# A quarter of wq's odd rows loaded behind wq's main part, by transfers of 95 and 33 partitions

## The chip, the cores and the metric

The kernel runs on one core of a Trainium2 chip. The metric is the device time of one execution in microseconds; the figure for a kernel is the median over several rounds. Profiled executions are single executions with the hardware profiler on.

## The reference

One decode step of a transformer block: layer norm, attention of one query token over a window of a cache, projection and residual, then layer norm, a gated feed-forward part with a relu gate, and residual. Four sequences, D = 576, 32 query heads on 16 key/value heads, head size 128, a window of 4096 positions, F = 4608, all in bf16.

```python
def _A_ref(x, k_cache, v_cache, wq, wo):
    W = min(4096, max(256, Sk // 4))                       # 4096
    q = (x @ wq).reshape(B, 1, 32, 128).transpose(0, 2, 1, 3)
    k = jnp.repeat(k_cache[:, :, Sk - W:, :], 2, axis=1)
    v = jnp.repeat(v_cache[:, :, Sk - W:, :], 2, axis=1)
    p = _softmax(jnp.einsum("bhqd,bhkd->bhqk", q, k) * (128 ** -0.5))
    o = jnp.einsum("bhqk,bhkd->bhqd", p, v)
    return o.transpose(0, 2, 1, 3).reshape(B, 1, 32 * 128) @ wo

def _B_ref(x, W_gate, W_up, W_down):
    gate = x @ W_gate
    return ((gate * (gate > 0)) * (x @ W_up)) @ W_down

h = A_x + _A_ref(_layernorm(A_x), A_k_cache, A_v_cache, A_wq, A_wo)
out = h + _B_ref(_layernorm(h), B_W_gate, B_W_up, B_W_down)
```

## The kernel before

Every input is read once: about 160 MB, of which 134 MB are K and V. The work on K and V is cut into 16 quads, each of one sequence and four key/value heads. A quad of K or of V is one transfer of 128 partitions with 32 KB each.

**Buffers.** All big inputs go through one SBUF tensor, `pool`, with four slots of 32 KB a partition. The helper `add` (from line 204) appends a transfer to the list `transfers` and notes who used the same bytes before it; the transfer waits for those users. Slots are handed out in turn to K0, K1, V0, K2, V1, K3 and so on.

**wq.** `wq` has 576 rows of 4096 columns. Rows 0 to 511, the main part, go as one transfer of 128 partitions with 32 KB each into slot 2 (`("wq", 0)`, line 237). Rows 512 to 575, called the odd rows here, are cut in halves of 2048 columns, so that they fill 128 partitions with 4 KB each: row r, half u stands in partition 2r + u. They go at the beginning of slot 3 (`("wq", 4)`, line 235) and are the first transfer in the list. V0 takes slot 2 and K2 slot 3 afterwards, and so both wait for the query projection (`QMM`).

**SP issues the list in order** (`prog_sync`): odd rows, main part, K0, K1, V0, K2 and so on, then `wo`, the gate and up weights, and six transfers of W_down. An issue whose buffer isn't free holds up all issues behind it. The sixteen DMA engines of the core work off what SP has issued, one row after the other; each transfer has a semaphore, which its engines raise as their shares land. x alone is issued by ACT.

**PE** (`prog_pe`, loop at line 483) computes the query projection in five blocks of contraction, the odd rows first (`c == 4`), then the four blocks of the main part. Each block is eight matmuls of 512 columns, and the accumulation over the five blocks ends with `QMM`. The first matmul of block 4 waits for the landing of the odd rows and for `XN41`, the normalized x that goes with them; the first of block 0 waits for the main part. ACT then copies the result into `q_bf` (line 311), and DVE transposes that (line 427, behind the first K transpose on line 403), from which the queries of the quads are made.

**The quads.** DVE transposes K in four parts (line 403), PE multiplies it with the queries, DVE and ACT make the softmax, PE multiplies with V, DVE collects. K2's and later loads wait for the transposes of the K that stood there, V's slots for the matmuls with V.

Line 466 is the helper for a matmul that loads its weights, line 468 the one for a matmul that keeps them.

Of the kernel before, what the change touches and what calls it, by code (L numbers as in the profile page):

```python
# [30 lines left out]
QUAD = NS * WIN * DH // 128  # L31
# [70 lines left out]
def bass_sequential_preLN__sliding_block_cached__glu_gated_reglu__decode_kernel(  # L102
# [12 lines left out]
    with ExitStack() as es:  # L115
        cnt = [0]

        def sb(name, shape, dt):
            return es.enter_context(nc.sbuf_tensor(name, shape, dt))

        pool = sb("pool", [128, NSLOT * QUAD], BF16)
# [79 lines left out]
        transfers = []  # L201
        at = {}

        def add(name, key, off, n, consumer, make):

            free = []
            for u in list(users):
                if u[0] < off + n and off < u[1]:
                    if u[2] not in free:
                        free.append(u[2])  # L210
                    if off <= u[0] and u[1] <= off + n:
                        users.remove(u)
            users.append((off, off + n, consumer))
            at[name] = off
            transfers.append((name, key, free, lambda e: make(e, pool[:, off:off + n])))
# [7 lines left out]
        def add_K(i):  # L223
            x = next(slots) % NSLOT
            add(("K", i), f"slot{x}", x * QUAD, QUAD, ("TR", 4 * i + 3),
                lambda e, o: e.dma_start(out=o, in_=quad(A_k_cache, i)))

        def add_V(i):
            x = next(slots) % NSLOT
            add(("V", i), f"slot{x}", x * QUAD, QUAD, ("PV", i),  # L230
                lambda e, o: e.dma_start(out=o, in_=quad(A_v_cache, i)))

        HQ = H * DH

        add(("wq", 4), "wq4", 2 * QUAD + 4 * HQ, HQ // 2, "QMM",
            lambda e, o: e.dma_start(out=o, in_=A_wq[512:576, :].rearrange("r (u n) -> (r u) n", u=2)))
        add(("wq", 0), "wq0", 2 * QUAD, 4 * HQ, "QMM",
            lambda e, o: e.dma_start(out=o, in_=A_wq[0:512, :].rearrange("(p u) n -> p (u n)", u=4)))
        for m in range(NQUAD + VLEAD):
            if m < NQUAD:  # L240
                add_K(m)
            if m >= VLEAD:
                add_V(m - VLEAD)
        add(("wo",), "wo", 0, EO * D, "ATTN",
            lambda e, o: e.dma_start(out=o, in_=A_wo.rearrange("(p e) n -> p (e n)", e=EO)))
        for k, (kind, W) in enumerate((("wg", B_W_gate), ("wu", B_W_up))):
            add((kind, 0), f"{kind}0", GU0 + 4 * k * ROW, 4 * F, None,
                lambda e, o, W=W: e.dma_start(out=o, in_=W[0:512, :].rearrange("(p u) n -> p (u n)", u=4)))
            add((kind, 4), f"{kind}4", GU0 + 8 * ROW + k * HALF, HALF, None,
                lambda e, o, W=W: e.dma_start(out=o, in_=W[512:576, :].rearrange("r (u n) -> (r u) n", u=2)))  # L250
# [3 lines left out]
        for k, (f0, f1) in enumerate(WD):  # L254
            transfers.append((("wd", k), f"wd{k}", ["ATTN"],
                              lambda e, f0=f0, f1=f1: e.dma_start(
                                  out=pool[:, f0 * D:f1 * D], in_=B_W_down.rearrange("(p j) n -> p (j n)", j=JJ)[:, f0 * D:f1 * D])))
# [4 lines left out]
        def land(name):  # L262
            return ("L",) + (name if isinstance(name, tuple) else (name,))
# [195 lines left out]
        def prog_pe(S):  # L459
            t = "tensor"  # L460

            def mm(o, l, r, start, stop, deps=(), name=None, skip=False, held=False):

                def make(e):
                    if not held:
                        return e.matmul(o, lhsT=l, rhs=r, start=start, stop=stop, skip_group_check=skip)  # L466
                    tile = tuple(next(x for x in (32, 64, 128) if x >= n) for n in (l.shape[0], l.shape[-1]))
                    return e.add_instruction(mybir.InstMatmult(  # L468
                        name=nc.get_next_instruction_name(), start_tensor_calc=start, stop_tensor_calc=stop, bass_skip_group_check=skip,
                        tile_size=tile, tile_position=(0, o.offset // o.ap[0][0] % 128), ldweights=False,  # L470
                        ins=[e.lower_ap(r), e.lower_ap(l)], outs=[e.lower_ap(o)]))

                S.op(t, make, deps=deps, name=name, signal=name is not None)
# [8 lines left out]
            mm(pb[STB][:, 0:B], dup[:, :], x4[:, :], True, True, deps=["D_X4", "DUP"], name="XDUP")  # L482
            for c in (4, 0, 1, 2, 3):
                s = at[("wq", 0)] + c * HQ if c < 4 else at[("wq", 4)]
                deps = [land(("wq", 0)), "D_XNT"] if c == 0 else [land(("wq", 4)), "XN41"] if c == 4 else []
                for g in range(4):
                    x0 = s + (g if c < 4 else g % 2) * 1024
                    for k in range(2):
                        mm(pb[QB[k]][32 * g:32 * g + 32, :], xnT[:, c, :] if c < 4 else xn4[:, g // 2, :], pool[:, x0 + 512 * k:x0 + 512 * k + 512], c == 4, c == 3,
                           deps=deps, name="QMM" if c == 3 and g == 3 and k == 1 else None, skip=True, held=k == 1)  # L490
                        deps = []
            for g in range(4):
                mm(pb[g][:, 0:128].rearrange("p (x h b) -> p x h b", x=4, b=B), sel[32 * g:32 * g + 32, :, :].rearrange("p g k -> p (g k)"),
                   qT[32 * g:32 * g + 32, :].rearrange("p (h x b) -> p x h b", x=4, b=32)[:, :, :, 0:B], True, True,
                   deps=["D_QT", "SEL"] if g == 0 else [], name="QREP" if g == 3 else None)
# [57 lines left out]
            for q in range(4):  # L553
                mm(pb[0][:, 0:EO * B], spread[:, q, :, :].rearrange("p h k -> p (h k)"), o_bf[:, q * EO:(q + 1) * EO, :].rearrange("p e b -> p (e b)"), q == 0, q == 3,
                   deps=["NORM", "SPREAD"] if q == 0 else [], name="OSEL" if q == 3 else None)
            for e_ in range(EO):
                deps = [land(("wo",)), "OX"] if e_ == 0 else []
                for u in range(2):
                    c0 = at[("wo",)] + e_ * D + u * HD
                    mm(attn[:, u * HD:(u + 1) * HD], oX[:, e_, :], pool[:, c0:c0 + HD], e_ == 0, e_ == EO - 1,  # L560
                       deps=deps, name="ATTN" if e_ == EO - 1 and u == 1 else None, held=u == 1)
                    deps = []
# [10 lines left out]
            for u, kind in ((0, "wg"), (1, "wu")):  # L573
                if u == 1:
                    residual()
                for c in range(4):
                    s = at[(kind, 0)] + c * F
                    deps = [land((kind, 0))] + (["N2"] if c == 0 and u == 0 else [])
                    for k, (f0, f1) in enumerate(CUTS):
                        for q in range(4):  # L580
# [3 lines left out]
                            deps = []  # L584
                s = at[(kind, 4)]
                deps = [land((kind, 4)), "HN41"]
                for k, (f0, f1) in enumerate(CUTS):
                    for q in range(4):
                        x0 = s + (q % 2) * FQ
                        mm(pb[GUB[u][k]][32 * q:32 * q + 32, 0:(f1 - f0) * JJ], hn4[:, q // 2, :], pool[:, x0 + f0 * JJ:x0 + f1 * JJ],  # L590
                           False, True, deps=deps, name=(("GATE", "GU")[u], k) if q == 3 else None, skip=True, held=k > 0)
                        deps = []

            for k, (f0, f1) in enumerate(WD):
                deps = [land(("wd", k))]
                for f in range(f0, f1):
                    if f % (JJ // 2) == 0:
                        deps = deps + [("HHT", f // (JJ // 2))]
                    for u in range(2):
                        last = f == FC - 1  # L600
                        mm(down(u), hhT[:, f, 0:B], wd_sb[:, f, OUTS[u][0]:OUTS[u][1]], False, last,
                           deps=deps, name="DOWN1" if last and u == 1 else None, skip=True)
                        deps = []

        progs = [("gpsimd", prog_pool), ("sync", prog_sync), ("scalar", prog_act), ("vector", prog_dve), ("tensor", prog_pe)]
        S.begin(False)
        for _, p in progs:
# [32 lines left out]
```

## Time and profile before

| | |
|---|---|
| median of 3 runs | 377.71 us (377.62 to 377.88) |
| profiled execution | 378.56 us |
| its span, first to last instruction | 377.2 us |
| PE matmul busy | 302.2 us, 80% of the span |
| DVE busy | 225.8 us, 60% |
| ACT busy | 53.4 us, 14% |
| read from HBM | 159.58 MB, 423 GB/s over the span |
| q1 (the queue of SP's transfers) | 98.8% of 16 engines' span |
| TensorE clock granted, mean | 0.923 |

The profiled execution's own time is 1.36 us above its span. A share of the DMA queue is the time that its packets took, over sixteen engines times the span. A DMA row of the issue list gives the median time from the issue by SP to the landing; most of it is time in which the transfer stands behind others. The packet records of the trace have the start, length and size of each packet of the DMA engines, but not the engine's number.

### The profile page before, as it was taken

Reading aid. Unit: us, or ns where it says so; the run is one execution under the profiler, and the core shown is the slowest. Engines: PE = TensorE matmul, PEld = TensorE weight load, DVE = VectorE, ACT = ScalarE, POOL = GpSimd, SP = SyncE. Lnnn points to the kernel's source line nnn. Section 1 sums busy time; section 2 is a strip of 40 time slices with the busy share of each in tenths; the row PEclk is TensorE's granted clock in tenths of the full one; section 3 lists DMA queues with packets and bytes.
Section 4 is the critical chain, followed back from the end, with each engine's and each line's share of the span. In section 5 each row is a group of like instructions: output and inputs, shape, how many; then the busy total and the mean of one; then the engine's idle time right before and its main releaser. Section 6 shows DMA issues by size and latency. Waiting matters only on the chain.

```text
span 377.2 us, 2603 instructions
## 1 busy us (share of the span) xinstructions
PE 302.2 (80%) x1432; PEld 73.0 (19%) x772; DVE 225.8 (60%) x165; ACT 53.4 (14%) x140; POOL 5.2 (1%) x15
## 2 busy tenths in 40 slices
PE   0509299969996999499969996899879996968667
PEld 0101022212221222022212221122112121212214
DVE  8046677595849493858476846666675768231230
ACT  2202402110220112002200220020202010101020
POOL 5000000000000000000000000000000000000000
PEclk9999789998999899989989997799959998996988
DMA  8999999999999999999999999999999999999996
GB/s 334 445 445 389 445 440 393 445 440 438 422 424 441 438 434 408 441 441 427 413 440 441 431 427 427 440 434 427 420 441 440 417 424 441 422 432 429 443 404 255
DMA packets 6506, 159.74 MB, mean 423 GB/s; under 512 B 728, under 2 KB 864, under 8 KB 1632
## 3 DMA queue, kind: packets, MB, share of 16 engines
q1 hardware_dynamic: 6488, 159.59, 98.8%
q8 instruction: 8, 0.13, 0.1%
q10 hardware_dynamic: 8, 0.00, 0.0%
q14 instruction: 2, 0.02, 0.0%
HBM read 159.58 MB, written 0.00 MB: 423 GB/s over the span
## 4 chain that ended last, share of the span: by engine, by line
DMA 47%; DVE 29%; PE 20%; ACT 3%; SPq 1%; issue 1%; DVEq 0%
DMA pool<-in_A_k_cache_dram 41%; DVE kT L403 20%; PE sc L466 7%; PE sc L468 6%; DMA pool<-in_B_W_down_dram 5%; DVE acc L420 4%; PE val L466 3%; PE val L468 3%; DVE own_sb L417 2%; DVE probT L414 2%; ACT P L338 2%; PE pb L466 1%; DVE o_bf L442 0%; ACT L338 0%; DVE rmx L406 0%
## 5 line engine op out<-in xcount | busy, mean ns | idle before, releaser
L403 DVE STREAM_TRANSPOSE kT<-pool 128x2048 f32<-128x2048 f32 x64 | 142.8, 2278 | 25.3 <-DMA pool<-in_A_k_cache_dram 24.3
L466 PE MATMUL sc<-kT,qz 128*128 128x512 bf16 x256 | 110.5, 432 | 36.6 <-DVE kT L403 36.3
L468 PE MATMUL sc<-kT,qz 128*128 128x512 bf16 x256 | 109.6, 428 | 0.0
L466 PE MATMUL val<-pool,probT 128*64 128x512 bf16 (+2 forms) x328 | 104.2, 374 | 4.4 <-DMA pool<-in_B_W_down_dram 4.4
L468 PE MATMUL val<-pool,probT 128*64 128x512 bf16 x256 | 96.2, 379 | 0.0
L466 PEld LDWEIGHTS sc<-kT,qz 128*128 128x128 bf16 x256 | 26.7, 104 | 146.5 <-issue 71.1
L466 PEld LDWEIGHTS val<-pool,probT 128*64 128x64 bf16 (+1 forms) x328 | 32.1, 107 | 81.3 <-issue 68.5
L406 DVE TENSOR_REDUCE rmx<-sc 128x1 f32<-128x1024 f32 x16 | 19.6, 1225 | 41.0 <-PE sc L468 41.0
L333 ACT ACTIVATE diag<-spot,rmx 128x16 f32<-128x16 f32 x16 | 4.9, 307 | 234.0 <-DVE rmx L406 234.0
L414 DVE STREAM_TRANSPOSE probT<-P 128x1024 bf16<-128x1024 bf16 x16 | 19.9, 1246 | 21.0 <-ACT P L338 21.0
L338 ACT ACTIVATE P<-sc,bias 128x1024 bf16<-128x1024 f32 x16 | 17.8, 1114 | 21.0 <-DVE bias L409 21.0
L327 ACT COPY qz<-qrep 32x128 bf16<-32x128 bf16 x64 | 18.8, 294 | 0.6
L409 DVE TENSOR_REDUCE bias<-pb 128x1 f32<-128x16 f32 x16 | 2.8, 175 | 23.8 <-PE pb L466 23.8
L420 DVE TENSOR_REDUCE acc<-own_sb 128x128 f32<-128x1024 f32 x8 | 15.2, 1897 | 0.3
L417 DVE TENSOR_TENSOR own_sb<-val,mask 128x1024 f32<-128x1024 f32 x8 | 9.6, 1200 | 7.9 <-PE val L468 7.9
L466 PE MATMUL sc<-pool,oX 128*4 128x288 bf16 x32 | 10.0, 338 | 0.4 <-ACT oX L347 0.4
L468 PE MATMUL sc<-pool,oX 128*4 128x288 bf16 x32 | 9.9, 336 | 0.0
L478 PE MATMUL pb<-ident_b,xn_bf 4*128 4x4 bf16 (+1 forms) x5 | 0.4, 180 | 10.0 <-DVE xn_bf L371 10.0
L466 PE MATMUL sc<-qT,sel 32*128 32x128 bf16 x4 | 0.3, 284 | 9.6 <-DVE qT L427 9.6
L445 DVE TENSOR_TENSOR h_row<-sc,x_bf 4x576 f32<-4x576 f32 x1 | 0.7, 745 | 11.6 <-PE sc L468 11.6
L466 PE MATMUL pb<-diag,same 128*128 128x16 f32 x32 | 6.3, 273 | 1.7 <-ACT diag L333 1.7
L466 PEld LDWEIGHTS pb<-diag,same 128*128 128x128 f32 x32 | 4.8, 188 | 11.8 <-ACT diag L333 7.4
(102 smaller groups left out, 85.7 us busy)
## 6 DMA issues: line engine op xcount, KB each, us to landing
pool<-in_A_k_cache_dram SPq DMA_DIRECT2D x16, 4096.0 KB, 26.8
pool<-in_A_v_cache_dram SPq DMA_DIRECT2D x16, 4096.0 KB, 26.4
pool<-in_A_wo_dram SPq DMA_DIRECT2D x1, 4608.0 KB, 18.3
pool<-in_B_W_gate_dram SPq DMA_DIRECT2D x1, 4608.0 KB, 18.6
pool<-in_B_W_up_dram SPq DMA_DIRECT2D x1, 4608.0 KB, 24.7
pool<-in_A_wq_dram SPq DMA_DIRECT2D x1, 4096.0 KB, 12.7
pool<-in_B_W_down_dram SPq DMA_DIRECT2D x1, 2016.0 KB, 15.0
pool<-in_B_W_down_dram SPq DMA_DIRECT2D x1, 1296.0 KB, 17.7
```

The source lines that it names most:

```text
L327: S.op(a, lambda e, src=src, dst=dst: e.copy(out=dst, in_=src), deps=deps, name=("QZ", i) if g == 3 else None, signal=g == 3)
L333: S.op(a, lambda e, i=i: e.activation(out=diag[:, i % 2, :], in_=spot[:, :], func=ACT.Copy, scale=rmx[:, i % 2:i % 2 + 1]), deps=[("RMAX", ...
L338: S.op(a, lambda e, i=i: e.activation(out=Pb[:, (i % 2) * 1024:(i % 2 + 1) * 1024], in_=sc[:, (i % 2) * 1024:(i % 2 + 1) * 1024], func=ACT ...
L403: S.op(v, lambda e: e.transpose(out=dst, in_=src), deps=deps, name=("TR", f))
L406: S.op(v, lambda e: e.tensor_reduce(out=rmx[:, i % 2:i % 2 + 1], in_=sc[:, (i % 2) * 1024:(i % 2 + 1) * 1024], axis=AX.X, op=ALU.max), dep ...
L409: S.op(v, lambda e: e.tensor_reduce(out=bias[:, i % 2:i % 2 + 1], in_=pb[TPB][:, 16 * (i % 2):16 * (i % 2) + 16], axis=AX.X, op=ALU.min), ...
L414: S.op(v, lambda e: e.transpose(out=pT[i % NPT], in_=Pb[:, (i % 2) * 1024:(i % 2 + 1) * 1024]), deps=[("EXP", i)] + ([("PV", i - NPT)] if ...
L417: S.op(v, lambda e: e.tensor_tensor(out=own_sb[:, :].rearrange("p (x d) -> p x d", d=DH), in0=val[:, :].rearrange("p (x d) -> p x d", d=DH ...
L420: S.op(v, lambda e: e.tensor_reduce(out=acc[:, w % 2, :], in_=own_sb[:, :].rearrange("p (x d) -> p d x", d=DH), axis=AX.X, op=ALU.add), de ...
L445: S.op(v, lambda e: e.tensor_tensor(out=h_row[:, :], in0=attn, in1=x_bf[:, :], op=ALU.add), deps=["ATTN", land("x")], name="H")
L466: return e.matmul(o, lhsT=l, rhs=r, start=start, stop=stop, skip_group_check=skip)
L468: return e.add_instruction(mybir.InstMatmult(name=nc.get_next_instruction_name(), start_tensor_calc=start, stop_tensor_calc=stop, bass_ski ...
```

## The change

The odd rows' first transfer is narrowed from 2048 to 1536 columns of each half (4 KB to 3 KB a partition). The remaining 512 columns (1 KB a partition, 128 KB in all) are loaded behind the main part and ahead of K0, by two transfers: partitions 0 to 94, and partitions 95 to 127. They go to the same place in SBUF as before. The two share one semaphore. The first matmul of block 4 waits for both as well as for the narrowed one. No computation is changed; no other transfer changes its place relative to the rest.

```diff
-        add(("wq", 4), "wq4", 2 * QUAD + 4 * HQ, HQ // 2, "QMM",
-            lambda e, o: e.dma_start(out=o, in_=A_wq[512:576, :].rearrange("r (u n) -> (r u) n", u=2)))
+        wq_odd = A_wq[512:576, :].rearrange("r (u n) -> (r u) n", u=2)
+        OW = HQ // 2
+        OA = OW - 512
+        add(("wq", 4), "wq4", 2 * QUAD + 4 * HQ, OA, "QMM",
+            lambda e, o: e.dma_start(out=o, in_=wq_odd[:, 0:OA]))
         add(("wq", 0), "wq0", 2 * QUAD, 4 * HQ, "QMM",
             lambda e, o: e.dma_start(out=o, in_=A_wq[0:512, :].rearrange("(p u) n -> p (u n)", u=4)))
+        o0 = 2 * QUAD + 4 * HQ + OA
+        add(("wq", 5), "wq5", o0, 512, "QMM", lambda e, o: e.dma_start(out=o[0:95, :], in_=wq_odd[0:95, OA:OW]))
+        transfers.append((("wq", 6), "wq5", [], lambda e: e.dma_start(out=pool[95:128, o0:o0 + 512], in_=wq_odd[95:128, OA:OW])))
         for m in range(NQUAD + VLEAD):
...
-                deps = [land(("wq", 0)), "D_XNT"] if c == 0 else [land(("wq", 4)), "XN41"] if c == 4 else []
+                deps = [land(("wq", 0)), "D_XNT"] if c == 0 else [land(("wq", 4)), land(("wq", 6)), "XN41"] if c == 4 else []
```

## The prediction

> **What bounds the kernel now.** I read the page in the order DMA rows, chain, waits, issues, then the trace's DMA packet and landing records for the one thing that the page does not separate: the sixteen DMA engines. First the page's slices and queues, and the table of stretches:
>
> ```profile
> DMA  8999999999999999999999999999999999999996
> DMA packets 6506, 159.74 MB, mean 423 GB/s; under 512 B 728, under 2 KB 864, under 8 KB 1632
> q1 hardware_dynamic: 6488, 159.59, 98.8%
> q8 instruction: 8, 0.13, 0.1%
> q10 hardware_dynamic: 8, 0.00, 0.0%
> q14 instruction: 2, 0.02, 0.0%
> ...
> 22.00:62.00 40.00, 27.23 (x106) 6.09 (x58) 26.07 (x17) 9.41 (x24) 0.00 (x0) 0.91 0.99 420
> 62.00:120.00 58.00, 51.93 (x220) 11.92 (x113) 42.73 (x27) 7.76 (x21) 0.00 (x0) 0.97 1.01 433
> 120.00:325.00 205.00, 179.79 (x728) 41.06 (x381) 136.37 (x84) 25.07 (x67) 0.00 (x0) 0.92 1.00 431
> ```
>
> The engines of queue q1 never stop between the first row (1.75 us) and the last (374.7 us): 98.8% of sixteen engines' span. PE (302 us) and DVE (226 us) are below that. The chain's end and the waits say the same:
>
> ```profile
> DMA 47%; DVE 29%; PE 20%; ACT 3%; SPq 1%; issue 1%; DVEq 0%
> ...
> 353.78 20.18 DMA pool<-in_B_W_down_dram
> 373.95 0.04 issue
> 374.00 0.70 PE val L466 x7
> 374.70 0.02 issue
> 374.72 0.68 PE val L466 x5
> 375.40 0.02 issue
> 375.42 0.42 DVE out_sb L456
> ```
>
> The last 20 us are a wait for W_down's rows. After the last landing (375.03 us) come two matmuls, a copy and the output, 2.2 us in all. So the end is set by the slowest engine's own list of packets. The engines do not finish together. These are the sixteen part-landings (us) of the last W_down transfer, from the trace's semaphore records:
>
> ```
> 373.16 373.17 373.22 373.23 373.25 373.37 373.73 374.04
> 374.65 374.66 374.68 374.73 374.75 374.76 374.78 375.03
> ```
>
> For K0, at the start, the spread was only 23.28 to 23.62. Each of q8's eight 16 KB packets (56.6, 97.7, 145.0, 188.6, 240.9, 284.6, 331.5 and 360.4 us) throws one engine back, about 1.55 us, each time another one: eight late engines. Seven land at 374.65 to 374.78; one, which already lagged 0.41 us, is last.
>
> **The price of a row**, from the packet records: rows of 2304 B follow each other on an engine at 89.5 ns, rows of 1152 B at 47 ns, so 4.5 ns a row and 0.0369 ns a byte. That is 42 ns for the new 1 KB row and 118 ns for a 3 KB row; the old 4 KB row is measured at 155 ns. A landing packet costs 6 ns.
>
> **wq4's columns 1536 to 2047 leave the first transfer.** Every engine carries eight of its rows: 8 x (155.3 - 117.6) = 0.30 us less for each of the sixteen.
>
> **The two new transfers** bring 128 rows of 1 KB. How 95 and 33 rows are dealt to engines no row shows. Bounds: sixteen even shares (8 or 9 rows and two landing packets, 0.35 to 0.39 us) net +0.05 to +0.09 us; all 128 rows on one late engine net 128 x 0.042 - 0.30 = +5.1 us; none on a late engine, -0.30 us. Nearest are the transfers of 128 rows (8 on each of 16) and x's 4 rows: q10's eight packets are one row and one landing packet on each of four engines. All are equal shares. With equal shares 95 goes as 5 x 19 and 33 as 11 x 3, and I take these. An engine with both carries 22 rows and nets 22 x 42.2 + 12 - 301 = +0.64 us; one with 19 rows nets +0.51; one with 3 rows, -0.17; one with none, -0.30. On the path counts only what the last engine gets. If the five loaded engines are early ones, they have 1.4 us or more in hand (373.25 against 374.65) and absorb 0.64. The last engine then gains 0.17 or 0.30, and its followers 0.25 us ahead gain at least 0.17, so they don't take over. I take **-0.25 us**.
>
> [...]
>
> Which five are they? Two of x's engines can be followed from their landing packets (ends 1.944 and 2.013 us) to their first wq row (1.941 and 2.010) and on, and as far as equal times allow it, neither is among those that the first four 16 KB packets hit. [...]
>
> **SP's queue.** Two more issues stand between wq's main part and K0; an issue there took 0.39 to 0.6 us, so K0 and K1 are issued about 1 us later. K0 was issued 11.8 us and K1 21 us before their first row's turn. Cost nothing; even at 3 us each it would be covered. No other queue changes place.
>
> **The new wait on PE.**
>
> ```profile
> 11.82 0.62 PE L466 MATMUL val<-pool,xn 128*32 128x512 bf16 x4 [0.97 <-ACT xn L308]
> 13.89 0.62 PE L466 MATMUL val<-pool,xnT 128*32 128x512 bf16 x4 [1.02 <-DMA pool<-in_A_wq_dram]
> 17.55 0.54 SPq L231 DMA_DIRECT2D pool<-in_A_v_cache_dram  x1
> 23.64 2.31 DVE L403 STREAM_TRANSPOSE kT<-pool 128x2048 f32<-128x2048 f32 x1 [13.70 <-DMA pool<-in_A_k_cache_dram]
> 25.88 1.20 DVE L427 STREAM_TRANSPOSE qT<-q_bf 128x1024 bf16<-128x1024 bf16 x1
> SPq L231 <- PE pb L468: 14.7, 1, 14.7
> ```
>
> The odd rows' matmuls, first in PE's order, now wait for both new transfers. These follow wq0, whose part-landings of 13.46 to 13.85 come 0.30 earlier; then 22 rows, 0.94 us: landed at 14.1 to 14.5 instead of PE starting at 11.82. All 40 matmuls queue behind (1.7 + 3.6 us, from 11.82 to 13.5 and 13.89 to 17.5), so they end near 19.7, 2.2 later. Two parties wait for them. The copies on ACT (17.56 to 18.63) move to about 20.8, but the transpose that reads them stands behind the first K transpose and starts at 25.88: 5 us in hand. SP's issue of V0 and, behind it, K2 moves from 17.55 to about 19.7; the engines reach V0 at 33.15: 13 us in hand. If either cover were gone the price would be 2.2 us.
>
> **K0's landing** moves by up to +0.64 on the loaded engines and -0.3 on others, and the first K transpose with it, by at most about 0.6 us. Buffers then free later by as much; the tightest issue I found, wo at 319.43 us, was 5.7 us ahead of its turn (325.12). Cost nothing.
>
> **Traffic settling.** Between 20 and 62 us the 32 KB rows, 1213 ns undisturbed, took longer by 0.88 us per engine in all; from 62 to 120 us hardly any of that is left, and later rows are 3 to 4 ns longer each. Setting five engines 0.8 to 0.95 us apart from the others may change this. Bounds: all of it saved, -0.9; doubled, +0.9. I take 0, since no row tells the sign.
>
> **Sum:** -0.25 against the profiled execution's 378.56 us (span 377.2 and 1.36 around it): 378.3. The median of the timed runs, 377.71, lies 0.85 below that execution; the forecast for the median is **377.45**. Within 0.2% (0.75 us, about what a measurement of this kernel can tell from no change) this is no change.
>
> **Rivals.**
> - *A loaded engine is a late one* (the other side). If the five include one of the seven at 374.78 or before, it ends at 375.42: +0.39, 378.1. If they include the last, +0.64, 378.35. It decides from the point where an engine's slack is under 0.64 less the relief. For it: eight of sixteen are late, so five engines drawn blind would nearly always include one. [...] Alone it stays just under 0.2%; with +0.15 from settling it passes.
> - *The settling changes*: by -0.5 or more on top of the forecast, 376.5 to 376.95 (faster by over 0.2%); or +0.5 and more on top of a late loaded engine, 378.5 to 379.2. For it: the loss is largest while the engines run close together. Against: the other eleven stay together.
> - *It does not do what it says*: even shares, +0.05 to +0.09: 377.8.
> - *A fixed price for each transfer.* W_down's last, 144 KB, lands 0.35 us after the one before: eight 1152 B rows at 47 ns are 0.38, so there is no gap between transfers. If each new transfer opened one of 1 us, +2: 379.7. [...] The 0.35 us speaks against it on a filled queue.
>
> **How the numbers follow.** Chances: relief as forecast 0.43, a loaded late engine 0.27 (of which 0.06 passes 0.2% with settling), even shares 0.08, settling beyond 0.2% faster 0.13 and slower 0.06, a fixed price or a bunch on few engines 0.03. Faster 0.13; slower 0.06 + 0.06 + 0.03 = 0.15; same 0.72. The range leaves out the far ends of settling and the fixed price: 376.8 to 378.5. The forecast's own range is 377.3 to 377.6.
>
> **What would show it.** Right: in the changed profile packets rise by 128 rows and some landing packets; the first K transpose starts at 23.3 to 24.3; the 40 matmuls end near 19.7; V0's issue near 19.7; the last landing 0.17 to 0.30 before 375.03, the spread of the last landings narrowed from 1.87 to about 1. Wrong: the last landing at 375.4 or later with a spread above 1.9 (late engines loaded), longer 32 KB rows between 20 and 62 us, or a gap on the queue around 13 us.

## The result and the profile after

The changed kernel takes 379.17 us (median of 6 runs, 378.70 to 379.91) against 377.68 us for the kernel before (377.57 to 377.88): a ratio of 1.0039 with a 95% interval of 1.0027 to 1.0051, so 1.5 us slower. Measured a second time beside other kernels it took 378.66 us, ratio 1.0029 (1.0017 to 1.0040). The forecast was 377.45 us with a range of 376.8 to 378.5; it was wrong in direction and range.

The profiled execution after took 379.02 us, with a span of 377.7. The page's slices and queues:

```profile
DMA  8999999999999999999999999999999999999995
DMA packets 6650, 159.74 MB, mean 423 GB/s; under 512 B 744, under 2 KB 1008, under 8 KB 1776
q1 hardware_dynamic: 6632, 159.59, 98.7%
q8 instruction: 8, 0.13, 0.1%
```

The queue is as full as before. Its packets rose from 6488 to 6632, by 144: 128 rows and 16 landing packets, which fits 5 + 11 engines for the two transfers. The start of the kernel in the timeline after:

```profile
15.86 0.62 PE L472 MATMUL val<-pool,xn 128*32 128x512 bf16 x4 [5.02 <-DMA pool<-in_A_wq_dram]
20.37 0.54 SPq L231 DMA_DIRECT2D pool<-in_A_v_cache_dram  x1
25.42 2.31 DVE L409 STREAM_TRANSPOSE kT<-pool 128x2048 f32<-128x2048 f32 x1 [15.49 <-DMA pool<-in_A_k_cache_dram]
27.66 1.20 DVE L433 STREAM_TRANSPOSE qT<-q_bf 128x1024 bf16<-128x1024 bf16 x1
```

PE's odd block starts at 15.86 us instead of 11.82, V0 is issued at 20.37 instead of 17.55, and the first K transpose starts at 25.42 instead of 23.64. None of this reaches the end by itself: V0's rows have their turn at about 33 us. What matters is why K0 is late. The view by stretches has a line for each window: its limits and length in us, five engines' busy time with their instructions, and in the last three columns granted clock, DMA share and GB/s. The kernel before:

```profile
12.00:18.00 6.00, 4.48 (x40) 0.60 (x16) 0.00 (x0) 0.44 (x1) 0.00 (x0) 1.00 0.96 415
18.00:60.00 42.00, 25.23 (x96) 5.62 (x53) 24.07 (x16) 9.59 (x25) 0.00 (x0) 0.92 1.00 421
```

The changed kernel:

```profile
12.00:18.00 6.00, 2.14 (x24) 0.57 (x16) 0.00 (x0) 0.00 (x0) 0.00 (x0) 1.00 0.94 360
18.00:60.00 42.00, 25.75 (x110) 5.31 (x55) 23.29 (x14) 8.21 (x20) 0.00 (x0) 0.92 1.01 435
```

From 12 to 18 us, where the two new transfers run and K0 begins, the DMA engines are nearly as busy (0.94 against 0.96) and move 360 GB/s instead of 415: 6 us x 55 / 433 = 0.76 us of transfer time lost over all engines. The view counts a row where it starts (360 GB/s is 62 rows of 32 KB and the 128 KB), so in so short a window one row is 5.5 GB/s and the figure is coarse. K0's sixteen part-landings say about the same without a window: on average they come at 24.20 us, and at 24.19 in a second profile of the change, against 23.38 and 23.46 in two profiles of the kernel before, so 0.7 to 0.8 us later. The end of the chain after:

```profile
352.29 15.61 DMA pool<-in_B_W_down_dram
367.90 0.04 issue
367.94 7.91 PE val L472 x55
375.85 0.02 issue
375.87 0.42 DVE out_sb L462
```

PE now follows the late first part of W_down without a gap, but its last two matmuls still wait for the last part. The sixteen part-landings (us) of that last transfer:

```
372.82 373.00 373.01 373.89 374.08 374.20 374.34 374.35
374.37 374.44 374.47 374.49 374.61 374.62 375.22 375.48
```

Fourteen engines end by 374.62, earlier than the late group before (374.65 to 374.78). Two stand alone at 375.22 and 375.48.

In all kernels that were profiled, the time is the last landing plus 3.50 to 3.54 us. So each result below can be read as first landing plus spread. The profile before is no good measure for half a microsecond: it stood 0.85 us above its median, and the stretch from 18 to 60 us, at 421 GB/s, is where its time went. The 32 KB rows that start there took 0.90 us per engine more than 1213 ns each, in the change's profile 0.15. A kernel below, e12_own, serves as its undisturbed stand-in.

### The profile page after: what moved, and what is told of

It is laid out like the page before. It is cut to its first block, busy times and chain, and to the rows that moved or that the text cites. A ratio compares the mean times of both kernels' runs of the same rounds, so it can differ in the third digit from the quotient of the medians.

```text
span 377.7 us, 2605 instructions
## 1 busy us (share of the span) xinstructions
PE 301.0 (80%) x1432; PEld 73.3 (19%) x772; DVE 225.7 (60%) x165; ACT 53.4 (14%) x140; POOL 5.2 (1%) x15
## 3 DMA queue, kind: packets, MB, share of 16 engines
q1 hardware_dynamic: 6632, 159.59, 98.7%
## 4 chain that ended last, share of the span: by engine, by line
DMA 45%; DVE 29%; PE 21%; ACT 3%; issue 0%; SPq 0%; DVEq 0%
DMA pool<-in_A_k_cache_dram 41%; DVE kT L409 20%; PE sc L472 7%; PE sc L474 6%; PE val L472 5%; DMA pool<-in_B_W_down_dram 4%; DVE acc L426 4%; PE val L474 3%; DVE own_sb L423 2%; DVE probT L420 2%; ACT P L344 2%; PE pb L472 1%; DVE o_bf L448 0%; ACT L344 0%; DVE rmx L412 0%
## 5 line engine op out<-in xcount | busy, mean ns | idle before, releaser
L472 PE MATMUL sc<-pool,oX 128*4 128x288 bf16 x32 | 9.2, 319 | 0.4 <-ACT oX L353 0.4
L474 PE MATMUL sc<-pool,oX 128*4 128x288 bf16 x32 | 9.2, 319 | 0.0
```

The lines of the kernel that those rows point to most:

```text
L474: return e.add_instruction(mybir.InstMatmult(name=nc.get_next_instruction_name(), start_tensor_calc=start, stop_tensor_calc=stop, bass_ski ...
```

## The experiments

All times are medians; "before" is the kernel before on the same chip.

| kernel | us | before | ratio, 95% interval | first landing + spread | GB/s, 12 to 18 us |
|---|---|---|---|---|---|
| e0_again (before) | 377.87 | 377.96 | 1.0000 (0.9992 to 1.0009) | 372.87 + 1.88 | 415 |
| change | 379.17 | 377.68 | 1.0039 (1.0027 to 1.0051) | 372.82 + 2.66 | 360 |
| e7_after (change) | 378.66 | 377.74 | 1.0029 (1.0017 to 1.0040) | 372.94 + 2.08 | 377 |
| e1_even | 378.39 | 377.96 | 1.0017 (1.0008 to 1.0025) | 372.60 + 2.29 | 388 |
| e2_ahead | 379.79 | 377.96 | 1.0051 (1.0038 to 1.0063) | 373.42 + 2.63 | 431 |
| e3_eighth | 378.29 | 377.96 | 1.0010 (1.0001 to 1.0019) | 372.65 + 2.11 | 399 |
| e4_long | 379.87 | 377.74 | 1.0051 (1.0038 to 1.0063) | 373.49 + 3.34 | 437 |
| e5_long2 | 379.43 | 377.74 | 1.0046 (1.0032 to 1.0059) | 374.11 + 2.13 | 437 |
| e6_swap | 378.16 | 377.74 | 1.0007 (0.9998 to 1.0016) | 372.52 + 2.18 | 437 |
| e8_one | 378.47 | 377.78 | 1.0015 (1.0006 to 1.0023) | 372.52 + 2.26 | 404 |
| e9_near | 378.43 | 377.78 | 1.0014 (1.0005 to 1.0022) | 372.95 + 2.16 | 388 |
| e10_five | 380.24 | 377.78 | 1.0061 (1.0048 to 1.0075) | 374.81 + 1.90 | 255 |
| e11_five2 | 382.47 | 377.78 | 1.0120 (1.0107 to 1.0134) | 375.42 + 3.40 | 221 |
| e12_own | 377.90 | 377.77 | 1.0003 (0.9994 to 1.0012) | 372.36 + 1.94 | 414 |
| e13_foreign | 378.73 | 377.77 | 1.0023 (1.0014 to 1.0032) | 373.27 + 1.93 | 386 |
| e14_own2 | 378.80 | 377.77 | 1.0024 (1.0015 to 1.0033) | 372.39 + 2.80 | 412 |

### First: is it the uneven shares or the place?

The first theory (A) was that five engines are set back and end last; its rival (B), that the later query projection or the extra transfers cost the time.

**e0_again**, the kernel before without an edit.

> The kernel before, unchanged, to see how much one profile of it differs from another. Time 377.7 within 0.2 us. All theories: the last W_down landing is spread by about 1.9 us over the sixteen engines, eight of them late by about 1.5 us. If the 32 KB rows' lost time between 20 and 62 us (0.88 us per engine in the first profile) is a matter of chance, this profile shows another sum or another place for it.

Its profiled execution took 378.27 us, again above its median. The spread was 1.88 as in the first profile. From 18 to 60 us it moved 432 GB/s instead of 421, and its 32 KB rows lost 0.65 us per engine instead of 0.90. In the profiles of the other kernels here they lost 0.02 to 0.19. Whether engines that stand further apart are spared this loss, or whether two executions happened to have it, is open: the medians of the kernel before lie 0.85 and 0.40 us below its two profiled executions.

**e1_even**

```diff
-o[0:95, :], in_=wq_odd[0:95, OA:OW]
+o[0:96, :], in_=wq_odd[0:96, OA:OW]
...
-pool[95:128, o0:o0 + 512], in_=wq_odd[95:128, OA:OW]
+pool[96:128, o0:o0 + 512], in_=wq_odd[96:128, OA:OW]
```

> The two late transfers cut as 96 and 32 partitions, which go in equal shares to sixteen engines (6 and 2 rows each); place, bytes, number of transfers and PE's later wait are as in the change. Theory A (uneven shares: five engines are set back and two of them end last): back to 377.7 within 0.3 us, spread of the last landing 1.9 us as before. Rival B (the place behind the main part, the later query projection or the two extra transfers cost the time): 379.2 as with the change.

Between both: 0.4 us over before, where the change on these chips is 0.9 to 1.5. Equal shares remove more than half of the loss, not all. The 1 KB rows took 58 ns on average, 13 of them over 100 ns.

**e2_ahead**: the two lines of the change for the quarter are moved ahead of `("wq", 0)`.

```diff
+        add(("wq", 5), "wq5", o0, 512, "QMM", lambda e, o: e.dma_start(out=o[0:95, :], in_=wq_odd[0:95, OA:OW]))
+        transfers.append((("wq", 6), "wq5", [], lambda e: e.dma_start(out=pool[95:128, o0:o0 + 512], in_=wq_odd[95:128, OA:OW])))
         add(("wq", 0), "wq0", 2 * QUAD, 4 * HQ, "QMM",
...
-        add(("wq", 5), "wq5", o0, 512, "QMM", lambda e, o: e.dma_start(out=o[0:95, :], in_=wq_odd[0:95, OA:OW]))
-        transfers.append((("wq", 6), "wq5", [], lambda e: e.dma_start(out=pool[95:128, o0:o0 + 512], in_=wq_odd[95:128, OA:OW])))
```

> The transfers of 95 and 33 partitions moved ahead of wq's main part; shares per engine as in the change, and the odd rows land near 5 us, so PE waits no longer than before. Theory A (uneven shares): still slower, 378.5 to 379.2, five engines late by 1 to 2 us from the start. Rival B (the later wait and projection): 377.4 to 377.8. Rival C (the 1 KB rows are slow only beside the 32 KB rows of K0): the 22 rows take 0.95 us instead of 1.3 to 2.1, and the time is 377.4 to 377.8 with the five engines late by 0.95.

Slower than any theory had it, 1.8 us over before. The odd rows had landed by 5.4 us, so rival B is out as the main cause. Rival C is out too: the rows took 51 ns on average, and it was the neighbours that suffered. The main part's 32 KB rows lost 0.84 us per engine before 10 us, and the first engine to finish wq's main part did so at 14.28 instead of 13.46 us.

**e3_eighth**

```diff
-        OA = OW - 512
+        OA = OW - 256
```

> As the change, with 256 columns instead of 512: 512 B rows, as many of them (22 on five engines). Theory A with a loss per byte: the five engines are set back by half, 0.7 to 1.0 us, time 378.0 to 378.4. Theory A with a loss per row: set back by 1.2 to 1.9 us, time 378.8 to 379.2. Rival B (place and wait): 379.2 as with the change.

0.3 us over before; the five last engines stood 0.6 to 1.0 us behind the first at K0. The time is in the range of a loss per byte (the interval reaches from nothing to 0.7 us), and outside that of a loss per row.

### Second: longer rows, and the change again

**e4_long** and **e5_long2** give the odd rows whole (4 KB) and first, in uneven shares. The edit of e4_long, against the kernel before:

```diff
-        add(("wq", 4), "wq4", 2 * QUAD + 4 * HQ, HQ // 2, "QMM",
-            lambda e, o: e.dma_start(out=o, in_=A_wq[512:576, :].rearrange("r (u n) -> (r u) n", u=2)))
+        add(("wq", 4), "wq4", o0, OW, "QMM", lambda e, o: e.dma_start(out=o[0:96, :], in_=wq_odd[0:96, :]))
+        for t, (r0, r1) in enumerate(((96, 121), (121, 128))):
+            transfers.append((("wq", 5 + t), "wq5", [], lambda e, r0=r0, r1=r1: e.dma_start(out=pool[r0:r1, o0:o0 + OW], in_=wq_odd[r0:r1, :])))
```

e5_long2 against e4_long:

```diff
-out=o[0:96, :], in_=wq_odd[0:96, :]
+out=o[0:64, :], in_=wq_odd[0:64, :]
-enumerate(((96, 121), (121, 128)))
+enumerate(((64, 89), (89, 114), (114, 128)))
```

> The kernel before, with wq's odd rows whole and first, cut as 96, 25 and 7 partitions of 4 KB: 12 rows on five engines, 7 on two more, 6 on the other nine, instead of 8 on each. In place and row length nothing else changes. Theory A (what counts is what the last engine of the run carries; the instruction packets set back others than the five): five engines later by 4 x 0.155 = 0.62 us, two earlier by 0.15, nine by 0.31; the two of the five that the 8 KB packets set back end near +1.5 of the first, the others near 1.56, so the spread of the last landings falls from 1.88 to about 1.6 and the time by 0.2 to 0.3 us. Rival D (uneven shares cost by themselves, wherever they fall): slower, 378.3 or more.

> As e4_long with a larger dose: 64, 25, 25 and 14 partitions of 4 KB, 15 rows on five engines, 5 on nine, 4 on two. Theory A: the five are later by 1.09 us, the others earlier by 0.47 or 0.62; two of the five end last, spread about 2.0 plus 0.5 between the groups, time within 0.3 us of before. Rival D: clearly slower than e4_long, 378.8 or more.

Both missed: 2.1 and 1.7 us over before, where theory A had a gain or nothing. Nor does rival D hold as put, since the larger dose cost no more. The loss lies from 2 to 12 us. The view by stretches for e4_long:

```profile
2.00:12.00 10.00, 0.79 (x10) 0.57 (x10) 7.62 (x19) 2.87 (x12) 3.71 (x6) 1.00 1.00 366
```

The kernel before:

```profile
2.00:12.00 10.00, 0.79 (x10) 0.57 (x10) 7.63 (x19) 2.88 (x12) 3.71 (x6) 1.00 1.04 440
```

74 GB/s less for 10 us is 1.7 us of transfer time, and K0 lands that much later on average (25.16 us). Here as in e2_ahead all engines are slowed while the small uneven transfers run beside the next large one: the main part's 32 KB rows lost 1.25 us per engine before 10 us. That was not in theory A and led to the third group of runs.

**e6_swap** issues the whole odd rows as one transfer behind the main part.

```diff
-        add(("wq", 4), "wq4", 2 * QUAD + 4 * HQ, HQ // 2, "QMM",
-            lambda e, o: e.dma_start(out=o, in_=A_wq[512:576, :].rearrange("r (u n) -> (r u) n", u=2)))
         add(("wq", 0), "wq0", 2 * QUAD, 4 * HQ, "QMM",
             lambda e, o: e.dma_start(out=o, in_=A_wq[0:512, :].rearrange("(p u) n -> p (u n)", u=4)))
+        add(("wq", 4), "wq4", 2 * QUAD + 4 * HQ, HQ // 2, "QMM",
+            lambda e, o: e.dma_start(out=o, in_=A_wq[512:576, :].rearrange("r (u n) -> (r u) n", u=2)))
```

> The kernel before, with the odd rows whole (4 KB, equal shares, one transfer) issued behind wq's main part: PE's odd block waits as long as in the change, SP's V0 and K2 issues are as late, but there are no 1 KB rows and no uneven shares. Theory A: as before, within 0.2 us. Rival B (what the even split lost is the place and the later wait): plus 0.4 us or more. If this is as before, the even split's loss belongs to its 1 KB rows or to two transfers instead of one.

0.4 us over before, with an interval that reaches from nothing to 0.6: not settled. From 12 to 60 us no transfer rate was lost (437 and 436 GB/s), but K0 landed 0.3 us later on average (23.74), with its engines spread over 0.66 us instead of 0.34.

**e7_after**, the change again.

> The changed kernel unchanged, for a second profile and its time beside the others of this chip. All theories: 1.0 to 1.5 us over the kernel before. Theory A: the spread of the last landings is again near 2.7 us, with two engines ahead of all others in lateness, which are two of the five that carry 22 of the 1 KB rows. If the rows' slow part (up to 300 ns each) is a matter of chance, the five engines' lag behind wq differs from the first profile's 1.3 to 2.1 us.

0.9 us over before, a little less than expected. The five engines stood 0.9 to 1.3 us behind at K0 (1.2 to 1.9 in the first profile), the rows took 59 ns on average (71). So both vary. Two engines again end last, but by less: 2.08.

### Third: the neighbours' loss

**e8_one** and **e9_near** take away the cut and the scattered source.

e8_one puts in place of the change's two transfers (PE waits for it in their place)

```diff
+        add(("wq", 5), "wq5", o0, 512, "QMM", lambda e, o: e.dma_start(out=o, in_=wq_odd[:, OA:OW]))
```

and e9_near reads from one stretch of memory:

```diff
+        near = A_wq[512:528, :].rearrange("r (u n) -> (r u) n", u=8)
-in_=wq_odd[0:95, OA:OW]
+in_=near[0:95, :]
-in_=wq_odd[95:128, OA:OW]
+in_=near[95:128, :]
```

> The last 512 columns of the odd rows behind the main part as one transfer of 128 partitions: 1 KB rows, eight on each engine. Theory E (the rows of all engines are slowed while a transfer cut otherwise than 128 over sixteen runs beside the next large one): no slowed rows near 13 us (the 96/32 cut lost 0.2 us per engine there, the change 0.3 to 0.5), time 377.7 to 378.0. Rival F (1 KB rows alone do it): the loss near 13 us as with 96/32, 378.3 or more.

> As the change, but the two late transfers read 128 KB that lie together in DRAM (rows 512 to 527 of wq in pieces of 1 KB) instead of 1 KB out of every 4; destination, shares and order are the change's. The odd rows' last quarter so has other values: the output is not the reference's, the work is the same. Rival G (the slow rows come from the scattered source): the rows take 46 ns each and the five engines lag 0.95 us behind wq, time 378.3 or less. Theory E (the destination or the uneven shares): slowed rows near 13 us as with the change, five engines late by 0.9 to 2.1 us, 378.5 to 379.2.

e9_near: for K0's rows the source is not it. Near 13 us they lost 0.39 us per engine, as much as with the change (0.34 and 0.29). For the 1 KB rows it may be a part: one of the 128 took over 100 ns, where the change had 14 and 6, and the five engines lagged by 0.8 to 1.0 us, as rival G has it. The time lies between the ranges of G and E.

e8_one: 1 KB rows in equal shares and one transfer took 47 ns, and K0's rows lost only 0.07 us, as theory E has it. Yet it took 0.7 us more than before. K0 landed at 23.81 us on average, 0.4 later than in the kernel before, with fifteen engines up to 0.73 us behind the first. The two engines that ended last, by 2.25 and 2.26 us, stood about 0.7 behind at K0 and were set back by about 1.5 by a 16 KB packet each. One engine stood 1.25 behind at K0, but it was still 1.27 behind at the end and not last. Part of the 0.4 us is older than the late transfer: the rows of wq's main part that start before 6 us lost 0.22 us per engine, and 0.14 to 0.32 in all six profiles in which a narrowed first transfer runs directly ahead of the main part, against 0.03 to 0.09 where the odd rows went first, whole and in one transfer. Why is open.

**e10_five** and **e11_five2** leave wq as it was and add rows of 24 KB on five engines, to space that nobody reads. PE's odd block waits for these rows too.

```diff
+        o0 = 2 * QUAD + 4 * HQ + HQ // 2
+        ballast = A_wq[0:15, :].rearrange("(p u) n -> p (u n)", u=3)
+        add(("wq", 5), "wq5", o0, 3 * HQ, "QMM", lambda e, o: e.dma_start(out=o[0:5, :], in_=ballast[0:5, :]))
```

In e11_five2 the ballast is twice as long, and a second transfer follows:

```diff
+        transfers.append((("wq", 6), "wq5", [], lambda e: e.dma_start(out=pool[5:10, o0:o0 + 3 * HQ], in_=ballast[5:10, :])))
```

> The kernel before, with wq untouched, and a transfer of five partitions of 24 KB added behind the main part, into space that nobody reads: one row of 0.91 us on each of five engines, no small rows, nothing moved. Theory A (the five have slack up to the last engine; the two that the 8 KB packets set back have 1.0 us): 377.7 to 378.1, the last landing within 0.2 us of before, spread 1.9. Rival D (any unevenness costs the whole run): plus 0.9 or more.

> As e10_five with two such transfers, 1.82 us more on each of the five engines. Theory A: the slack is used up; the two of the five that the 8 KB packets set back end at 0.9 + 1.8 = 2.7 us behind the first engine instead of 1.9, so plus 0.7 to 1.0 over before and 0.6 to 0.8 over the single dose: 378.5 to 378.8. Rival D: plus 1.8 or more, twice the single dose.

Far off: 2.5 and 4.7 us. But e10_five's spread is 1.90, as before: the last engines did not lag more; all sixteen were late. The 24 KB rows, priced at 0.91 us, took 2.15 to 2.31, and K0's rows lost 1.95 us per engine.

### Fourth: the same shares to other partitions

**e12_own** and **e13_foreign** differ from e10_five in the destination alone, and **e14_own2** from e11_five2. e12_own writes partitions 0, 4, 8, 12 and 16:

```diff
-out=o[0:5, :]
+out=o[0:17:4, :]
```

e13_foreign writes 0, 26, 52, 78 and 104:

```diff
-out=o[0:5, :]
+out=o[0:105:26, :]
```

e14_own2 writes those of e12_own and the ones beside them:

```diff
-out=o[0:5, :]
+out=o[0:17:4, :]
...
-out=pool[5:10, o0:o0 + 3 * HQ]
+out=pool[1:18:4, o0:o0 + 3 * HQ]
```

> As e10_five (five rows of 24 KB added behind the main part, for space that nobody reads), but to partitions 0, 4, 8, 12 and 16 instead of 0 to 4. [...] Theory Q (a transfer on few engines holds up the others wherever it writes): about 380.2 as e10_five.

> [...] Theory Q: about 380.2. [...]

> Two such transfers, to partitions 0, 4, 8, 12, 16 and to 1, 5, 9, 13, 17: 1.82 us more on each of five engines. [...] Theory Q: 382.5 as e11_five2.

The medians of 377.90, 378.73 and 378.80 us lie 2.3, 1.5 and 3.7 below theory Q's. e12_own's last landing, 374.30, was earlier than in both profiles of the kernel before (375.03 and 374.75). The view by stretches for e10_five:

```profile
12.00:18.00 6.00, 0.62 (x8) 0.33 (x8) 0.00 (x0) 0.00 (x0) 0.00 (x0) 1.00 0.99 255
```

For e13_foreign:

```profile
12.00:18.00 6.00, 2.42 (x24) 0.70 (x16) 0.00 (x0) 0.06 (x1) 0.00 (x0) 1.00 1.03 386
```

For e12_own:

```profile
12.00:18.00 6.00, 3.44 (x36) 0.91 (x20) 0.00 (x0) 0.00 (x0) 0.00 (x0) 1.00 0.96 414
```

Same bytes, shares, source and place: 255, 386 and 414 GB/s, and 2.5, 1.0 and 0.1 us over before. The rows took 2.15 to 2.31 us, 1.23 to 1.32 us, and 0.912 us each. K0's rows lost 1.95, 0.70 and 0.01 us per engine, and K0 landed at 26.07, 24.54 and 23.63 us on average. So a transfer on few engines costs nothing by itself (377.90 us against 377.77), and theory Q is out; the partitions that it writes decide, and they decide for the other engines too. How they decide was not shown: the trace has no record of which engine writes which partition.

e14_own2 then shows theory A without such a loss: the rate is 412 GB/s, the first landing is e12_own's (372.39 against 372.36), and the spread grows from 1.94 to 2.80. Its five engines at K0, and the last landings, as lags in us behind the first:

```
K0      0.00 ... 0.27 | 1.70 1.79 1.80 1.80 1.86
W_down  0.00 0.15 0.25 | 1.55 1.56 1.59 1.64 1.65 1.67 1.73 1.78 1.84 1.87 1.94 | 2.55 2.80
```

Two of the five jump between the landings at 72 and 82 us by 0.7 to 1.0 us, when the two 8 KB packets of queue q14 (81.7 and 82.9 us) run. None of the five is hit by a 16 KB packet (1.55 us); that would have shown as a lag of 3.2 or more. In e12_own the same jump takes two engines from 0.85 to 0.95 to 1.53 and 1.91, level with the late group, and so for nothing.

## Why the prediction was wrong

- **The shares were right**: 5 x 19 and 11 x 3 fit the 144 more packets, and the part-landings of the two transfers in the first profile of the change: six at 13.46 to 13.96 us, as of engines with 3 rows, and ten at 14.51 to 15.77, as two on each of the five with 22. Which five was an estimate: that x's engines are among them no run shows. In e14_own2 none of the five engines of a five-row transfer is hit by a 16 KB packet.
- **"On the path counts only what the last engine gets"** is the step that failed. It took the rows of one engine as no matter to the others. But all engines lost: K0's rows 0.34 and 0.29 us per engine in the two profiles of the change, beside engines that were serving the 1 KB rows. On average K0 landed 0.7 to 0.8 us later than in the kernel before. Against e12_own the first landing of W_down's last transfer came 0.46 and 0.58 us later, where the step had it 0.30 earlier. That the loss in the change is the one of e10_five is inferred: what the partitions do was shown with other rows, and for the change only the source (e9_near) and the uneven cut (e1_even, e8_one) were varied. Nor is it the whole: with equal shares (e1_even, e8_one) K0 still landed 0.4 us later, about half of the delay.
- **"0.30 us less for each of the sixteen"** was mis-sized too. The sixteen landings of wq's main part came at 13.55 and 13.72 us on average in the change, at 13.61 and 13.68 in the kernel before, so little or nothing of the relief was left there. The term took 155 ns for a 4 KB row; these first rows took 202 ns on average in the profile before, and behind the narrowed transfer the first rows of the main part lost 0.2 us more.
- **"Have 1.4 us or more in hand"** was wrong for two of the five. The 8 KB packets set two of the loaded engines back, so these two had 1.0 to 1.3 in hand. In the profile before, the part-landings show two engines that stand 0.6 and 1.0 us behind the first from the landing at 82 us on and land at 373.73 and 374.04. That these are two of the five is inferred from e12_own and e14_own2.
- **"Absorb 0.64"** was mis-sized: the 42 ns a row (46 in a record, since records overlap by 3 to 4 ns) became 71 and 59 in the records, and the five engines stood 1.2 to 1.9 and 0.9 to 1.3 us behind the first at K0 instead of 0.94 at most. With 0.7 to 1.0 more from the 8 KB packets, two ended last, by 2.66 and 2.08.
- **The wait on PE** was right in kind and 1.4 us short (15.86, predicted 14.1 to 14.5). The odd block was read too long: it ran from 11.82 to 12.87 us, not to 13.5. So the forecast end of 19.7 was near the measured 20.3 in part by luck. Its cover held: the copies end at 21.45, 4 us before the first K transpose, and V0 was issued 13 us before its turn. SP's extra issues cost nothing: K0 was issued at 2.39 us.
- **Traffic settling** did not cost the change anything. From 18 to 60 us its rows lost 0.15 us per engine in both profiles, against 0.90 and 0.65 in those of the kernel before. If that is an effect of the change it was a gain of 0.5 us or more, which the prediction had as a bound; the medians do not show whether it is.
- **The rivals.** "A loaded engine is a late one" had the right side and, in the first profile, near the right size, but by another packet, and it left the common loss out. A fixed price for each transfer is not seen: e12_own has one more transfer than the kernel before and no loss (377.90 us against 377.77).

The sum against e12_own's profile (last landing 374.30): first landing +0.46, spread +0.72, together +1.18 in the first profile of the change; +0.58 and +0.14, +0.72, in the second. The medians say 1.5 and 0.9.

No version here beats the kernel before. Giving engines with slack more of the odd rows cost 2.1 and 1.7 us in e4_long and e5_long2. In e12_own five engines carry 0.91 us more each at no cost, but no run here takes work off the late engines in that way.

## What to carry to other kernels

Where a kernel keeps the DMA queue full from start to end, price a transfer on all engines, not only on those that carry it: look at the GB/s of its stretch beside the DMA share. From 12 to 18 us e10_five had a share of 0.99 at 255 GB/s, e12_own 0.96 at 414. Beside a large transfer of 128 partitions, five rows to partitions 0 to 4 slowed both (2.15 to 2.31 us a row, and 1.95 us per engine lost by K0's rows); to partitions 0, 4, 8, 12, 16 they slowed neither (0.912 and 0.01). Before loading an engine for its slack, find every packet that it has yet to serve, the instruction packets too: in the first profile of the change two of the five ended last, with 0.7 to 1.0 us from 8 KB packets.

## What the runs showed of the hardware

- Five 24 KB rows beside K0's load: 0.912 us each to partitions 0, 4, 8, 12 and 16 (e12_own); 1.23 to 1.32 to 0, 26, 52, 78 and 104 (e13_foreign); 2.15 to 2.31 to 0 to 4 (e10_five). K0's rows lost 0.01, 0.70 and 1.95 us per engine.
- One 16 KB instruction packet set one DMA engine back by about 1.55 us in the profile before, one 8 KB packet by 0.6 to 1.0 there and by 0.7 to 1.0 in e14_own2. Nothing made it up later: at the last landing of the profile before, eight of sixteen engines stood 1.49 to 1.87 us behind the first, as eight 16 KB packets on eight different engines leave them.
- Between 18 and 60 us the 32 KB rows lost 0.90 and 0.65 us per engine in two profiles of the kernel before, at most 0.19 in the others. Left open are this, the loss of wq's first rows behind a narrowed transfer (0.14 to 0.32 us per engine), and e6_swap's 0.4 us.
